# A fused attention and feed-forward block: all first loads on SP's queue, q and k weights in one transfer, masks set as words, one memset left out

## The chip, the cores and the metric

The kernel runs on one core of one Trainium2 chip. The metric is the device time of one execution in microseconds. A core has five engines with an instruction stream each: TensorE (PE in the profile, its weight loads PEld), VectorE (DVE), ScalarE (ACT), GpSimd (POOL) and SyncE (SP, used here for issuing transfers). Transfers are carried out by 16 DMA engines; SP and ACT each have a queue of their own into them (SPq and ACTq in the profile).

## The reference

```python
x = A_x                                    # 1 x 2048 x 448, bf16
xn = _layernorm(x, axis=-1)
return x + _A_ref(xn, A_wqkv, A_wo) + _B_ref(xn, B_w_gate, B_w_up, B_w_down)

def _A_ref(x, wqkv, wo):                   # H = 16 heads of Dh = 28, window W = 256
    qkv = (lambda x, *d: x.transpose(*d))((x @ wqkv).reshape(B, S, 3, H, Dh), 2, 0, 3, 1, 4)
    q, k, v = qkv[0], qkv[1], qkv[2]
    scores = jnp.einsum("bhqd,bhkd->bhqk", q, k) * (Dh ** -0.5)
    mask = (idx[:, None] - idx[None, :] >= 0) & (idx[:, None] - idx[None, :] < W)
    ...
    return (lambda x, *d: x.transpose(*d))(o, 0, 2, 1, 3).reshape(B, S, D) @ wo

def _B_ref(x, w_gate, w_up, w_down):       # F = 1792
    return (_gelu(x @ w_gate) * (x @ w_up)) @ w_down
```

A layer norm of 2048 tokens with 448 features, then two branches from it: attention over a sliding window of 256 tokens, and a gated feed-forward layer. Both are added to the input.

## The kernel before

Tokens are cut into 16 tiles of 128 and into four blocks of 512 (`qb` 0 to 3). All weights stay in SBUF. A block runs through projection of q, k and v, attention (scores, exponential, masking, product with v), the gate and up products with the gelu between them, and the down product, which ends with the add of x and a store. The stages of neighbouring blocks are interleaved by a plan written out by hand; nothing is reordered by a scheduler, so each engine runs its instructions in the order in which the program states them, and each queue issues its transfers in that order.

The change touches the start. What happens there, with lines:

- Lines 85 to 98 issue the first loads. Tile 0 of x goes to SP's queue (L85), tile 1 to ACT's (L86), tiles 2 and 3 to SP's in one transfer (L87). The q and k weights (`wraw`, rows 0 to 383 of `A_wqkv`) come in parts: the first four heads of q and of k on ACT's queue (L89), the other twelve later on SP's (L97). Between them SP issues the v weights (`wv`, L90), the last 64 weight rows, twice, into both halves of the partitions (L92 for q and k, L94 for v), and tiles 4 to 7 of x (L95). The first part of the up weights (`wu`) follows (`load_ffn`, L82).
- Line 124 sets `warm` (the later home of `wo`) to zero in two memsets: the first 512 columns, which the warm-up matmuls read, and the rest. Line 134 sets the masks to 1.
- L717 runs nine matmuls on the zeros (`warmup(9)`), L729 a tenth.
- L718 to 739 take tiles 0 to 3 through statistics (L155, L156, VectorE), the inverse deviation (L160, L161, ScalarE), the normalisation (L170, VectorE) and the transpose (L184 and L186, TensorE; the copy out of PSUM L187, on ScalarE for tiles 0 to 2, on VectorE for tile 3). In between, the first v products run (L191), and the pad copies (L711) spread the first heads' weights from `wraw` to slots of 32 columns in `wqp` (VectorE) and `wkp` (ScalarE).
- L745 and 746 are the first q and k products, on all four tiles; L747 copies the last weight rows to `w3p`; L750 to 752 take the statistics of tiles 4 and 5; L244 and L245 copy q and k out; L652 and L656 are scores and exponential.

Further on, in `ahead3` (L778 to 797), SP issues a list of later loads: the gate weights, the rest of the up weights, tiles 12 to 15 of x in one transfer (L789), `wo` in eight, and the down weights (`wd`, L797) in four transfers of up to four row blocks.

Of the kernel before, what the change touches and what calls it, by code (L numbers as in the profile page):

```python
# [13 lines left out]
f32 = mybir.dt.float32  # L14
i32 = mybir.dt.int32

S, D, H, Dh, F = 2048, 448, 16, 28, 1792
P = 128
NT = S // P
NF = F // P  # L20
QB, NB = 512, 4
# [6 lines left out]
def kernel(  # L28
# [11 lines left out]
    nc = tc.nc  # L40
# [18 lines left out]
    xv = A_x.rearrange("b (n p) d -> p (b n) d", p=P)  # L59
# [3 lines left out]
    x_sb = const.tile([P, NT, D], bf16, name="x_sb")  # L63
    wv = const.tile([P, 4, D], bf16, name="wv")
    v_sb = const.tile([P, NT, H, 32], bf16, name="v_sb")
    wraw = blk.tile([P, 4, 2 * D], bf16, name="wraw", tag="hT")
# [5 lines left out]
    def rows(w, c0, n):  # L72
        return w[c0 * P:(c0 + n) * P, :].rearrange("(c p) n -> p c n", p=P)

    def load_ffn(dst, w, pairs):

        wv64 = w.rearrange("(c p) (h n) -> p c h n", p=64, h=2)
        ns = slice(pairs.start * P, pairs.stop * P)  # L80
        for hi in range(2):
            nc.sync.dma_start(out=dst[64 * hi:64 * hi + 64, :, ns], in_=wv64[:, :, hi, ns])  # L82

    wqk = rows(A_wqkv, 0, 3)[:, :, 0:2 * D]
    nc.sync.dma_start(out=x_sb[:, 0, :], in_=xv[:, 0, :])  # L85
    nc.scalar.dma_start(out=x_sb[:, 1, :], in_=xv[:, 1, :])  # L86
    nc.sync.dma_start(out=x_sb[:, 2:4, :], in_=xv[:, 2:4, :])  # L87
    for c in (0, D):
        nc.scalar.dma_start(out=wraw[:, 0:3, c:c + 4 * Dh], in_=wqk[:, :, c:c + 4 * Dh])  # L89
    nc.sync.dma_start(out=wv[:, 0:3, :], in_=rows(A_wqkv, 0, 3)[:, :, 2 * D:3 * D])  # L90
    for a in range(2):
        nc.sync.dma_start(out=wraw[64 * a:64 * a + 64, 3, 0:D], in_=A_wqkv[384:448, a * D:(a + 1) * D])  # L92
    for a in range(2):
        nc.sync.dma_start(out=wv[64 * a:64 * a + 64, 3, :], in_=A_wqkv[384:448, 2 * D:3 * D])  # L94
    nc.sync.dma_start(out=x_sb[:, 4:8, :], in_=xv[:, 4:8, :])  # L95
    for c in (0, D):
        nc.sync.dma_start(out=wraw[:, 0:3, c + 4 * Dh:c + D], in_=wqk[:, :, c + 4 * Dh:c + D])  # L97
    load_ffn(wu, B_w_up, slice(0, 5))

    ident = const.tile([P, P], bf16, name="ident")  # L100
# [7 lines left out]
    masks = const.tile([P, 3, 4, 64], bf16, name="masks")  # L108
# [11 lines left out]
    eps_t = const.tile([P, 1], f32, name="eps_t")  # L120
    nc.vector.memset(eps_t[:, :], 1e-5)
    warm = wo[:, :, :].rearrange("p g n -> p (g n)")
    for c in (slice(0, QB), slice(QB, 4 * D)):
        nc.vector.memset(warm[:, c], 0.0)
    wqp = const.tile([P, 3, H, 32], bf16, name="wqp")
    wkp = const.tile([P, 3, H, 32], bf16, name="wkp")
    w3p = const.tile([P, H, 32], bf16, name="w3p")
# [3 lines left out]
    nc.vector.memset(wqp[:, :, :, Dh:32], 0.0)  # L131
    nc.vector.memset(wkp[:, :, :, Dh:32], 0.0)
    nc.vector.memset(w3p[:, :, Dh:32], 0.0)
    nc.vector.memset(masks[:, :, :, :], 1.0)
    nc.scalar.preload_act_table_set("natural_log_exp_and_others")

    xnT = const.tile([P, 4, S], bf16, name="xnT")
# [27 lines left out]
    def norm(t):  # L165
        xn = work.tile([P, 4, P], bf16, name="xn", bufs=4)
        xf = xn[:, :, :].rearrange("p a b -> p (a b)")
        both = ((0, D, 0), (D, 64, 384))
        for lo, n, src in both if t > 3 else both[:1]:
            nc.vector.tensor_scalar(out=xf[:, lo:lo + n], in0=x_sb[:, t, src:src + n], scalar1=mv_all[:, t, 0:1],  # L170
                                    scalar2=rstd_all[:, t:t + 1], op0=ALU.subtract, op1=ALU.mult)
        xns[t] = xn

    def dma_transp(t):

        nc.sync.dma_start_transpose(out=xnT[:, :, t * P:(t + 1) * P], in_=xns.pop(t)[:, :, :].rearrange("p a b -> p (a b)"))
# [100 lines left out]
    def fill_pads(last):  # L277


        def put(dst, src, n, lo):  # L280

            src = src.rearrange("p (j d) -> p j d", d=Dh)[:, :, lo:]
            if n == 4:
                nc.gpsimd.tensor_copy(out=dst[:, 12:16, Dh:32], in_=src[:, :, 24:28])
            src = src[:, :, 0:24].rearrange("p j (g i) -> p g j i", i=8)[:, :, :, 0:4]
            nc.gpsimd.tensor_copy(out=dst[:, 0:12, Dh:32].rearrange("p (g j) i -> p g j i", j=4), in_=src)

        if not last:
            for c in range(3):
                k = wraw[:, c, D + 12 * Dh:2 * D]  # L290
                put(wqp[:, c, :, :], k, 4, 0)
                put(wkp[:, c, :, :], k, 3, 4)
            return
        put(w3p[0:64, :, :], w3k[0:64, :], 4, 0)
        put(w3p[64:128, :, :], w3k[64:128, :], 3, 4)
        nc.gpsimd.memset(w3p[64:128, 12:16, :], 0.0)
# [135 lines left out]
    def swap(qb, t=None, n=4):  # L432

        t0 = P * (4 * qb if t is None else t)
        to = t0 - qb * QB + ring(qb).start
        for hi in range(2):
            nc.sync.dma_start(out=xsw[64 * hi:64 * hi + 64, :, to:to + n * P],
                              in_=xnT[64 - 64 * hi:P - 64 * hi, 0:3, t0:t0 + n * P])

    def swap_weights():  # L440

        for hi, src in enumerate((wqp, wkp)):
            nc.sync.dma_start(out=wsq[64 * hi:64 * hi + 64], in_=src[64 - 64 * hi:P - 64 * hi, 0:3])
# [334 lines left out]
    def ahead3():  # L778
        for t in (5, 6, 7):
            norm(t)  # L780
            dma_transp(t)
        swap(1, 4, 2)
        swap(1, 6, 2)
        fill_pads(False)
        swap_weights()
        load_ffn(wg, B_w_gate, slice(0, 3))
        load_ffn(wg, B_w_gate, slice(3, 7))
        load_ffn(wu, B_w_up, slice(5, 7))
        nc.sync.dma_start(out=x_sb[:, 12:16, :], in_=xv[:, 12:16, :])  # L789
        wo_v = A_wo.rearrange("(g j d) n -> j d g n", g=4, j=4)  # L790
        tail = A_wo[14 * Dh:, :].rearrange("(t i) n -> i t n", i=4)
        for j, (t0, n) in enumerate(SLOTS):
            nc.sync.dma_start(out=wo[32 * j:32 * j + Dh, 0:n, :], in_=wo_v[j][:, 0:n])
            nc.sync.dma_start(out=wo[32 * j + Dh:32 * j + 32, 0:n, :], in_=tail[:, t0:t0 + n])
        for k in range(0, NF, 4):
            n = min(4, NF - k)
            nc.sync.dma_start(out=wd[:, k:k + n, :], in_=rows(B_w_down, k, n))  # L797

    for qb in range(NB):
# [4 lines left out]
        if qb == 0:  # L804
# [3 lines left out]
            w = gen_pairs(1, (("v", 0), ("v", 2), ("k", 0), ("k", 1), ("k", 2)))  # L808
            plan = [[(u, 2), ahead, (u, 1)], [lambda: v_dense(2, pvs[2]), (u, 2), ahead2, (u, 1)],
                    [lambda: spare.append(spare.pop(1)), (u, 2), ahead3, (u, 4)], [lambda: stat(8), (u, 11)],  # L810
                    [lambda: stat(9), (u, 7), lambda: stat(10), (u, 7), lambda: fill_pads(True)], ["sums", (u, 7)],
                    ["inverse", "scale", (w, 11)], [(w, 10)],
# [210 lines left out]
```

## Time and profile before

| | |
|---|---|
| device time, median of three runs | 214.37 us (214.35, 214.37, 214.7) |
| span of the profiled execution, first to last instruction | 213.1 us |
| mean granted TensorE clock | 0.996 |
| TensorE busy | 207.6 us, 97% |
| VectorE busy | 157.5 us, 74% |
| ScalarE busy | 131.6 us, 62% |
| GpSimd busy | 48.6 us, 23% |
| bytes moved by DMA | 15.67 MB, mean 74 GB/s |

For the profiled execution the span is known, not a device time of its own. The page has the busy time of each engine, the span in 40 slices, the DMA queues, the chain of work that ended last, and the costliest groups. Queries on the trace give the instructions in order of time, with the idle time of the engine ahead of each and what ended it in square brackets, and the busy time of chosen stretches. A row of SPq or ACTq is the time in which the queue's engine issues a transfer, not that in which the bytes move. Sizes in KB are units of 1024 bytes; GB/s are decimal.

### The profile page before, as it was taken

Reading aid. Unit: us, or ns where it says so; the run is one execution under the profiler, and the core shown is the slowest. Engines: PE = TensorE matmul, PEld = TensorE weight load, DVE = VectorE, ACT = ScalarE, POOL = GpSimd, SP = SyncE. Lnnn points to the kernel's source line nnn. Section 1 sums busy time; section 2 is a strip of 40 time slices with the busy share of each in tenths; the row PEclk is TensorE's granted clock in tenths of the full one; section 3 lists DMA queues with packets and bytes.
Section 4 is the critical chain, followed back from the end, with each engine's and each line's share of the span. In section 5 each row is a group of like instructions: output and inputs, shape, how many; then the busy total and the mean of one; then the engine's idle time right before and its main releaser. Section 6 shows DMA issues by size and latency. Waiting matters only on the chain.

```text
span 213.1 us, 6428 instructions
## 1 busy us (share of the span) xinstructions
PE 207.6 (97%) x2722; PEld 101.2 (47%) x2722; DVE 157.5 (74%) x355; ACT 131.6 (62%) x123; POOL 48.6 (23%) x86
## 2 busy tenths in 40 slices
PE   7999999999999999999999999999999999999992
PEld 2433444444454545444445445444445444544992
DVE  7899998999767985796536997495483898479531
ACT  4699578566777977423777887532676877665000
POOL 5287658451000220041000201022000022006001
PEclk9999999999999999999999999999999999999998
DMA  6999969979420101003421000001000101000011
GB/s 184 280 221 215 106 172 220 243 241 171 110 53 25 37 20 26 8 5 65 74 74 46 25 0 29 20 0 30 16 3 0 47 4 45 6 0 0 26 45 49
DMA packets 23993, 15.67 MB, mean 74 GB/s; under 512 B 9208, under 2 KB 23832, under 8 KB 23960
## 3 DMA queue, kind: packets, MB, share of 16 engines
q1 hardware_dynamic: 22918, 14.87, 31.2%
q8 instruction: 22, 0.36, 0.7%
q10 hardware_dynamic: 1042, 0.34, 0.7%
q14 instruction: 11, 0.09, 0.1%
HBM read 9.26 MB, written 2.41 MB: 55 GB/s over the span
## 4 chain that ended last, share of the span: by engine, by line
PE 94%; DVE 1%; ACT 1%; DMA 1%; issue 1%; DVEq 0%; ACTq 0%
PE po L393 26%; PE gt L456 20%; PE u L456 12%; PE ue L456 8%; PE pq L334 7%; PE sc L652 6%; PE ov L624 5%; PE pv L320 4%; PE pq L191 2%; PE pv L191 1%; DMA x_sb<-in_A_x_dram 1%; ACT p_sb L656 1%; DVE st L155 1%; PE s L191 1%; PE pk L191 1%
## 5 line engine op out<-in xcount | busy, mean ns | idle before, releaser
L656 ACT ACTIVATE p_sb<-sc 128x2048 bf16<-128x2048 f32 x39 | 73.2, 1878 | 20.5 <-PE sc L652 13.5
L496 ACT ACTIVATE p_sb<-gt 128x1024 bf16<-128x1024 f32 x28 | 28.7, 1025 | 33.6 <-PE gt L456 30.7
L591 POOL TENSOR_TENSOR oN<-oc,l 128x512 bf16<-128x512 f32 x16 | 21.5, 1355 | 120.0 <-DVE l L604 120.0
L393 PE MATMUL po<-wd,hT 128*128 128x448 bf16 (+1 forms) x266 | 46.2, 324 | 0.0
L456 PE MATMUL gt<-xnT,wg 64*128 64x512 bf16 x224 | 45.6, 376 | 0.0
L456 PE MATMUL gt<-xsw,wg 64*128 64x512 bf16 x168 | 40.7, 376 | 0.0
L504 DVE TENSOR_TENSOR hT<-p_sb,u 128x512 bf16<-128x512 bf16 x34 | 21.9, 677 | 16.0 <-PE u L456 15.8
L572 DVE TENSOR_TENSOR p_sb<-p_sb,masks 128x256 bf16<-128x256 bf16 (+1 forms) x90 | 27.8, 363 | 7.6 <-ACT p_sb L656 7.6
L393 PEld LDWEIGHTS <-hT 128*128 128x128 bf16 x266 | 24.5, 98 | 16.8 <-issue 2.2
L456 PEld LDWEIGHTS <-wg 64*128 64x128 bf16 x392 | 19.0, 94 | 22.5 <-issue 0.2
L456 PEld LDWEIGHTS <-wu 64*128 64x128 bf16 x392 | 18.7, 94 | 22.4 <-issue 0.8
L456 PE MATMUL u<-xnT,wu 64*128 64x512 bf16 x136 | 28.1, 376 | 0.0
L456 PE MATMUL u<-xsw,wu 64*128 64x512 bf16 x102 | 24.7, 376 | 0.0
L382 DVE TENSOR_TENSOR res<-po,x_sb 128x448 bf16<-128x448 f32 (+1 forms) x17 | 9.8, 592 | 11.6 <-PE po L393 9.3
L456 PE MATMUL ue<-xnT,wu 64*128 64x512 bf16 x88 | 18.0, 377 | 0.0
L652 PE MATMUL sc<-qT,kT 28*64 28x320 bf16 (+7 forms) x648 | 16.4, 261 | 0.1
L456 PE MATMUL ue<-xsw,wu 64*128 64x512 bf16 x66 | 16.4, 377 | 0.0
L582 POOL TENSOR_SCALAR_AFFINE_SELECT p_sb<-p_sb 128x512 bf16<-128x512 bf16 (+1 forms) x21 | 14.2, 702 | 6.6 <-ACT p_sb L656 6.5
L609 DVE TENSOR_TENSOR oc<-oc,ov 128x512 f32<-128x512 f32 x12 | 8.2, 681 | 8.7 <-ACT oc L608 8.7
L652 PEld LDWEIGHTS <-kT 28*64 28x64 bf16 (+1 forms) x648 | 7.5, 102 | 13.3 <-issue 12.0
L393 PE MATMUL po<-wo,oN 128*128 128x448 bf16 (+1 forms) x70 | 13.0, 320 | 0.0
L473 DVE CAST hT<-ue 128x512 bf16<-128x512 f32 x18 | 11.6, 679 | 1.9 <-PE ue L456 1.8
(108 smaller groups left out, 276.9 us busy)
## 6 DMA issues: line engine op xcount, KB each, us to landing
out_dram<-res SPq DMA_DIRECT2D x15, 112.0 KB
x_sb<-in_A_x_dram SPq DMA_DIRECT2D x3, 448.0 KB
wd<-in_B_w_down_dram SPq DMA_DIRECT2D x3, 448.0 KB
xsw<-xnT SPq DMA_DIRECT2D x6, 192.0 KB
wu<-in_B_w_up_dram SPq DMA_DIRECT2D x2, 560.0 KB
wg<-in_B_w_gate_dram SPq DMA_DIRECT2D x2, 448.0 KB
wg<-in_B_w_gate_dram SPq DMA_DIRECT2D x2, 336.0 KB
wraw<-in_A_wqkv_dram SPq DMA_DIRECT2D x2, 252.0 KB
```

The source lines that it names most:

```text
L334: nc.tensor.matmul(ps, lhsT=w.rearrange("p h d -> p (h d)"), rhs=xchunk(qb, hi, c, qb * QB, QB), start=c == 0, stop=c == 6, tile_position= ...
L393: nc.tensor.matmul(po[:, a:b], lhsT=x[:, k, tt * P:(tt + 1) * P], rhs=wt[:, k, lo + a:lo + b], start=start and n == a == 0, stop=stop and ...
L456: nc.tensor.matmul(ps, lhsT=w[64 * hi:64 * hi + 64, c, p * P:(p + 1) * P], rhs=xchunk(qb, hi, c, qb * QB, QB), start=c == 0, stop=c == 6, ...
L473: copy(out=hTs[qb][:, p + 7 * i, :], in_=us[i])
L496: nc.scalar.activation(out=ges[p][:, :, :], in_=gt[:, :, :], func=ACT.Gelu_apprx_tanh)
L504: nc.vector.tensor_tensor(out=hT[:, p + 7 * i, :], in0=ge[:, i, :], in1=u, op=ALU.mult)
L572: nc.vector.tensor_tensor(out=reg, in0=reg, in1=m, op=ALU.mult)
L582: nc.gpsimd.affine_select(out=reg, in_=reg, pattern=mid + [[1 if diag else -1, min(w, P)]], compare_op=ALU.is_ge, fill=0.0, base=0 if diag ...
L591: nc.gpsimd.tensor_tensor(out=oN[:, g, :], in0=oc[:, :], in1=inv, op=ALU.mult)
L624: nc.tensor.matmul(ov[half or 0][32 * j:32 * j + 32, q0:q0 + nq], lhsT=v_sb[r, kt, 4 * g + j, :], rhs=p_sb[r, j, col:col + nq], start=n == ...
L652: nc.tensor.matmul(ss[k0:k0 + nk, j, col:col + nq], lhsT=kT[r, g, kt * P + k0:kt * P + k0 + nk], rhs=qT[r, g, ring(qb).start + q0:ring(qb) ...
L656: nc.scalar.activation(out=p_sb[:, :, 0:ncol], in_=ss[:, :, 0:ncol], func=ACT.Exp, scale=SCALE)
```

## The change

The first loads all go to SP's queue: tile 0, tile 1, tiles 2 and 3, the v weights with their last rows, the q and k weights of rows 0 to 383 in one transfer of whole rows (1792 bytes a row in place of pieces of 224 and 672), their last rows, then tiles 4 and 5, 6 and 7. The masks are set as 32-bit words that hold two bf16 ones each. The second memset of `warm` goes. Later on, tiles 12 to 15 come in two transfers, and the down weights in five, of up to three row blocks.

```diff
     nc.sync.dma_start(out=x_sb[:, 0, :], in_=xv[:, 0, :])
-    nc.scalar.dma_start(out=x_sb[:, 1, :], in_=xv[:, 1, :])
+    nc.sync.dma_start(out=x_sb[:, 1, :], in_=xv[:, 1, :])
     nc.sync.dma_start(out=x_sb[:, 2:4, :], in_=xv[:, 2:4, :])
-    for c in (0, D):
-        nc.scalar.dma_start(out=wraw[:, 0:3, c:c + 4 * Dh], in_=wqk[:, :, c:c + 4 * Dh])
     nc.sync.dma_start(out=wv[:, 0:3, :], in_=rows(A_wqkv, 0, 3)[:, :, 2 * D:3 * D])
     for a in range(2):
+        nc.sync.dma_start(out=wv[64 * a:64 * a + 64, 3, :], in_=A_wqkv[384:448, 2 * D:3 * D])
+    nc.sync.dma_start(out=wraw[:, 0:3, :], in_=wqk)
+    for a in range(2):
         nc.sync.dma_start(out=wraw[64 * a:64 * a + 64, 3, 0:D], in_=A_wqkv[384:448, a * D:(a + 1) * D])
-    for a in range(2):
-        nc.sync.dma_start(out=wv[64 * a:64 * a + 64, 3, :], in_=A_wqkv[384:448, 2 * D:3 * D])
-    nc.sync.dma_start(out=x_sb[:, 4:8, :], in_=xv[:, 4:8, :])
-    for c in (0, D):
-        nc.sync.dma_start(out=wraw[:, 0:3, c + 4 * Dh:c + D], in_=wqk[:, :, c + 4 * Dh:c + D])
+    for t in (4, 6):
+        nc.sync.dma_start(out=x_sb[:, t:t + 2, :], in_=xv[:, t:t + 2, :])
     load_ffn(wu, B_w_up, slice(0, 5))
...
-    for c in (slice(0, QB), slice(QB, 4 * D)):
-        nc.vector.memset(warm[:, c], 0.0)
+    nc.vector.memset(warm[:, 0:QB], 0.0)
...
-    nc.vector.memset(masks[:, :, :, :], 1.0)
+    nc.vector.memset(masks[:, :, :, :].rearrange("p a b c -> p (a b c)").bitcast(f32), 1 + 0x3F80 / 2**23)
...
-        nc.sync.dma_start(out=x_sb[:, 12:16, :], in_=xv[:, 12:16, :])
+        for t in (12, 14):
+            nc.sync.dma_start(out=x_sb[:, t:t + 2, :], in_=xv[:, t:t + 2, :])
...
-        for k in range(0, NF, 4):
-            n = min(4, NF - k)
+        for k in range(0, NF, 3):
+            n = min(3, NF - k)
             nc.sync.dma_start(out=wd[:, k:k + n, :], in_=rows(B_w_down, k, n))
```

## The prediction

> **What bounds the kernel now.** I read the page's shares first, then the busy time of the stretch in which TensorE works, then the chain of waits from the front, then the engines' first rows in order of time. In the second answer the columns are the stretch, its length, busy time by engine with instruction counts, granted clock, DMA share and GB/s.
>
> ```profile
> PE 207.6 (97%) x2722; PEld 101.2 (47%) x2722; DVE 157.5 (74%) x355; ACT 131.6 (62%) x123; POOL 48.6 (23%) x86
> ```
> ```profile
> 1.40:209.60 208.20, 207.54 (x2722) 101.14 (x2722) 157.13 (x352) 131.62 (x123) 47.12 (x78) 1.00 0.33 75
> ```
>
> Between 1.4 and 209.6 us TensorE is busy for all but 208.20 - 207.54 = 0.66 us. Transfers, VectorE and ScalarE therefore cannot win time by being faster in the body of the kernel; there they can only lose it, by being late. One stretch hides more than that row shows, because matmuls without use count as busy: the start.
>
> ```profile
> 0.82 2.45 DMA x_sb<-in_A_x_dram
> ...
> 3.29 0.64 DVE st L155
> ```
> ```profile
> 1.39 4.02 PE L150 MATMUL wps<-wo 128*128 128x512 bf16 x9 [1.39 <-DVE wo L124]
> 5.20 0.53 PE L184 MATMUL tp<-ident,xn 128*128 128x128 bf16 x3
> ...
> 5.91 0.61 PE L150 MATMUL wps<-wo 128*128 128x512 bf16 x1
> 6.31 0.40 PE L184 MATMUL tp<-ident,xn 128*128 128x128 bf16 x3
> 6.64 0.25 PE L186 MATMUL tp<-ident,xn 128*64 128x128 bf16 x2
> 6.99 0.74 PE L191 MATMUL pv<-wv,xnT 128*128 128x448 bf16 x3
> ```
> ```profile
> 9.05 0.33 PEld L191 LDWEIGHTS <-wqp 128*128 128x128 bf16 x3 [0.29 <-DVE xnT L187]
> ```
>
> The chain opens with the load of x tile 0: issued at 0.82, landed 2.45 us later, at 3.27. From there VectorE normalises four tiles in a row. TensorE runs nine matmuls that nobody reads, from 1.39 on, then transposes each tile as it comes. It meets its last visible wait at 9.05, for the copy of tile 3's transpose. So in this kernel a change of the first loads is worth what it does to the time of that 9.05, and nothing else.
>
> ```profile
> 1.06 0.94 DVE L124 MEMSET wo<- 128x256 uint32 x2
> 2.37 0.70 DVE L134 MEMSET masks<- 128x768 bf16 x1
> 3.29 0.63 DVE L155 BATCH_NORM_STATS2 st<-x_sb 128x6 f32<-128x448 bf16 x1 [0.23 <-DMA x_sb<-in_A_x_dram]
> 4.05 0.59 DVE L155 BATCH_NORM_STATS2 st<-x_sb 128x6 f32<-128x448 bf16 x1
> 5.06 0.62 DVE L155 BATCH_NORM_STATS2 st<-x_sb 128x6 f32<-128x448 bf16 x1
> ...
> 7.84 0.27 DVE L711 COPY wqp<-wraw 128x336 bf16<-128x336 bf16 x1
> 8.57 0.42 DVE L187 COPY xnT<-tp 128x512 bf16<-128x512 bf16 x1 [0.46 <-PE tp L186]
> 9.10 0.62 DVE L155 BATCH_NORM_STATS2 st<-x_sb 128x6 f32<-128x448 bf16 x1
> 10.91 0.69 DVE L245 CAST kT<-s 128x512 bf16<-128x512 f32 x1 [0.24 <-PE s L197]
> ```
>
> These are VectorE's rows. Only the first statistics row waits for a transfer, and for 0.23 us.
>
> **The change, part by part.** *The memsets.* The two of L124 set 256 + 640 words in 0.94 us; the 640 go, which by words is 0.94 x 640 / 896 = 0.67 us. The masks' 768 halves become 384 words; at 0.94 / 896 us a word that is 0.40 in place of 0.70 us. VectorE is then free at about 3.07 - 0.67 - 0.30 = 2.1 us rather than at 3.07. By itself this is worth nothing: the load of x tile 0 covers it. But it is needed for the next part, since with VectorE busy until 3.07 an earlier tile could win 0.22 us at most. The first memset, which releases TensorE at 1.39, is the same.
>
> *Tile 1 and the weights leave ACT's queue.*
>
> ```profile
> 0.82 0.42 ACTq L86 DMA_DIRECT2D x_sb<-in_A_x_dram  x1
> 1.27 1.01 ACTq L89 DMA_DIRECT2D wraw<-in_A_wqkv_dram  x2
> 2.31 1.28 ACT L135 ACT_TABLE_LOAD   x1 [2.31 <-issue]
> 4.17 0.29 ACT L160 ACTIVATE lnv<-mv_all,eps_t 128x1 f32<-128x1 f32 x1 [0.58 <-DVE mv_all L156]
> ```
> ```profile
> 0.82 0.39 SPq L85 DMA_DIRECT2D x_sb<-in_A_x_dram  x1
> 1.27 0.42 SPq L87 DMA_DIRECT2D x_sb<-in_A_x_dram  x1
> 1.74 0.47 SPq L90 DMA_DIRECT2D wv<-in_A_wqkv_dram  x1
> 2.24 1.21 SPq L92 DMA_DIRECT2D wraw<-in_A_wqkv_dram  x2
> 3.50 1.23 SPq L94 DMA_DIRECT2D wv<-in_A_wqkv_dram  x2
> 4.77 0.59 SPq L95 DMA_DIRECT2D x_sb<-in_A_x_dram  x1
> ```
>
> Today tiles 0 and 1 are issued in the same moment from two queues and share the engines. Afterwards tile 0 has them alone. ScalarE's table load ends at 3.59 now and its first work starts at 4.17, so the 1.5 us of issuing it is spared is covered. What tile 0 gains, no row shows. The nearest is a store of the same 112 KB at the kernel's quiet end, where the result buffer's next writer waits for it:
>
> ```profile
> 204.88 3.89 SPq L384 DMA_DIRECT2D out_dram<-res  x4
> ```
> ```profile
> 206.73 0.62 DVE L382 TENSOR_TENSOR res<-po,x_sb 128x448 bf16<-128x448 f32 x1 [1.11 <-DMA out_dram<-res]
> ```
>
> That is 1.85 us from issue to use. So tile 0 lands between 0.82 + 1.85 = 2.67 (a gain of 0.6) and 3.27 (none, if the 2.45 is the latency of a first load). I take 3.0, a gain of 0.27, nearer the middle: the load shares with 112 KB only, and the stream is slow then (133 GB/s in the row of 1.5 to 2.5 us below).
>
> The Trainium skill, "DMA: Bandwidth & Descriptors", section "Queues, rings and completion order", says that each DMA engine takes turns between the queues that have work for it, a packet at a time. By it tile 1 delays tile 0 today, which is the gain taken here; how much, the two rows above must say. The same page, "Issuing engines are not separate DMA queues", speaks against the change: issuing from several engines saves issue time and nothing else. By it the change gives up one issue step for tile 1 and gains nothing in bandwidth; the sum would then be that of the first rival, no gain. The rows of before cannot tell the two apart.
>
> Tile 1 is now issued second on SP, at 1.27. With 1.85 to 2.45 us it lands at 3.1 to 3.7; VectorE wants it at 4.05 - 0.27 = 3.78. Tiles 2 and 3 go to 1.74 and are wanted at 5.06 - 0.27 = 4.79, 3 us later. Neither is waited for.
>
> *Weights in one transfer.* This is the part that can lose. VectorE's pad copy (7.84) reads the first heads of the q weights. They came early, in 168 KB; now the whole 672 KB must land, behind four x tiles, the v weights and their two halves. SP's steps are 0.45, 0.47 and 0.50 us and, for transfers of 64 rows, (4.77 - 3.50) / 2 = 0.63, so the seventh transfer is issued at 0.82 + 2 x 0.45 + 0.47 + 0.50 + 2 x 0.63 = 3.95. Bytes up to its end: 448 + 336 + 112 + 672 KB = 1568 KB = 1.606 MB.
>
> ```profile
> 1.50:2.50 1.00, 1.00 (x3) 0.32 (x3) 0.89 (x5) 0.19 (x1) 1.00 (x2) 1.00 0.56 133
> 2.50:3.50 1.00, 1.00 (x4) 0.31 (x3) 0.77 (x2) 1.00 (x1) 1.00 (x2) 1.00 1.01 305
> 3.50:5.50 2.00, 2.00 (x8) 0.72 (x6) 1.93 (x6) 1.09 (x5) 0.17 (x1) 1.00 1.06 298
> 7.00:9.00 2.00, 2.00 (x16) 1.05 (x16) 1.22 (x5) 1.82 (x5) 0.00 (x0) 1.00 1.11 354
> 11.00:18.00 7.00, 6.88 (x54) 2.55 (x53) 6.43 (x17) 6.57 (x9) 6.00 (x17) 1.00 1.12 229
> ```
>
> By 2.5 us 0.133 MB are through. The other 1.473 MB take 4.16 us at 354 GB/s, 4.94 at 298, 6.43 at 229. To the last byte I add 0.45 us until the landing is seen: tiles 0 and 1, 0.229 MB, are through at 2.5 + 0.096 / 0.305 = 2.82, and tile 0 counts as landed at 3.27. So the weights land at 7.1, 7.9 or 9.4. I take 7.9, from the row of the same kind of transfers. The pad copy may slip until 8.57 - 0.27 = 8.30 before it holds up the copy of tile 3, since VectorE idles 0.46 us there; with the gain of 0.27 that is 8.03. So nothing is lost at 7.9, with 0.13 us to spare. Issue is not the limit: at 298 GB/s the 0.918 MB ahead end at 5.1, after the weights' issue.
>
> Behind them come the last weight rows (112 KB) and tiles 4 and 5 (224 KB): 1.95 MB, by the same working 2.5 + 6.1 + 0.45 = 9.05, wanted at 9.10 - 0.27 = 8.83. VectorE then is 0.22 us late, and the row at 10.91 has 0.24 us of idle time to take it. If that cover is gone, the scores, which need this cast, start later one for one. The loads behind (tiles 6 and 7, the up weights) have the same bytes ahead of them as before.
>
> *Later splits.* Tiles 12 to 15 in two, the down weights in five rather than four: two more issues of about 0.5 us on SP.
>
> ```profile
> 43.02 2.05 SPq L797 DMA_DIRECT2D wd<-in_B_w_down_dram  x4
> 45.17 8.58 SPq L176 DMA_TRANSPOSE xnT<-xn  x4
> ```
> ```profile
> 52.73 2.76 PE po L393 x14
> ```
>
> The down weights are issued until 45.1 and first read at 52.73; one step more leaves over 7 us. Behind them on SP stand the four transposes of tiles 8 to 11, the first at 45.17; their issue is spread over 8.58 us, so an added 0.5 us at its front is small against the gaps between them. Price: none, and 0.5 us if something in that list has no slack after all.
>
> **The sum**, against the profiled span of 213.1: -0.27 at the first tile, 0 for memsets, table load, tile 1 and later splits, +0.05 for weights that come just late: -0.22, span 212.9. The three runs have a median of 214.37, 1.27 more than the span; what lies outside it does not change. Forecast 214.15.
>
> **The rivals.** *Nothing is gained* (0.18): the 2.45 us is latency, tile 1 cost tile 0 nothing; for it, tile 0 is the first load of all; against it, two loads of 112 KB in one moment at 133 GB/s. Time 214.37, with the weights still in time. *The weights come late* (0.20): the one mechanism that ends slower. It needs a landing after 8.30 plus 0.43, that is a mean rate below 1.473 / (8.73 - 0.45 - 2.5) = 255 GB/s from 2.5 us on; for it, 229 in the row from 11 to 18 us and the skewed finish of many engines; against it, that row carries loads into 64 partitions each, these go into 128. At 8.9 the price is 0.6 us: 214.97; at 9.4, 1.1. *The tile comes much sooner* (0.22): landing at 2.67 as the store does. VectorE is free at 2.1, so its whole chain moves by 0.6. TensorE's nine matmuls still end at about 5.2 and the tenth at 6.3, so the v product at 6.99 can come no earlier than the last transposes ahead of it allow, which go at 6.64, so about 6.75; but the waits between 7 and 9.05 close too, and 9.05 moves by 0.45 to 0.55: 213.87, if the weights land by 7.9. *TensorE is the limit* of any gain belongs to the forecast: it caps 6.99 at 0.24, not 9.05.
>
> **How the numbers follow.** Forecast 0.40, no gain 0.18, late 0.20, much sooner 0.22. A change within 0.2% of 214.37, that is 0.43 us, cannot be told from none here. The forecast and the no-gain case lie inside it: same 0.58, faster 0.22, slower 0.20. The forecast's own range is 213.95 to 214.4. The range of 8 in 10 reaches into both outer cases: 213.8 to 214.9.
>
> **What would show it.** In the changed profile the first statistics row should start at 3.0 (2.7 to 3.3) with a longer wait for x_sb ahead of it; the pad copy of wqp should show no wait for wraw, or one whose size gives the loss; the weight load at 9.05 should stand near 8.8; the statistics row of tile 4 should not wait over 0.25 us. I am wrong if 9.05 moves by more than 0.5 us either way, or if it moves and the end does not.

## The result and the profile after

The changed kernel takes 215.86 us (median of 8 executions, 215.35 to 218.48), the kernel before beside it 214.53 us (8 executions, 214.35 to 215.18). The ratio is 1.0073, with a 95% interval of 1.0046 to 1.0099: 1.0 to 2.1 us slower. Forecast were 214.15 us, and 213.8 to 214.9 as the range. One execution of the experiments below, the 219.31 us of e8, was in a slower state and is left out of its ratio.

The head of the page after, and its busy times:

```profile
span 213.7 us, 6426 instructions
...
PE 207.9 (97%) x2722; PEld 101.3 (47%) x2722; DVE 156.7 (73%) x354; ACT 131.6 (62%) x123; POOL 48.5 (23%) x86
```

TensorE does the same work. What has moved is the start. First VectorE's rows in order of time (start, duration, line, operation; in brackets the idle time before it and what ended it):

```profile
1.61 0.38 DVE L131 MEMSET masks<- 128x384 f32 x1
2.83 0.63 DVE L152 BATCH_NORM_STATS2 st<-x_sb 128x6 f32<-128x448 bf16 x1 [0.83 <-DMA x_sb<-in_A_x_dram]
...
3.89 0.63 DVE L152 BATCH_NORM_STATS2 st<-x_sb 128x6 f32<-128x448 bf16 x1 [0.22 <-DMA x_sb<-in_A_x_dram]
...
9.35 0.28 DVE L708 COPY wqp<-wraw 128x336 bf16<-128x336 bf16 x1 [1.55 <-DMA wraw<-in_A_wqkv_dram]
9.54 0.41 DVE L184 COPY xnT<-tp 128x512 bf16<-128x512 bf16 x1
9.87 0.27 DVE L744 COPY w3p<-wraw 128x448 bf16<-128x448 bf16 x1
...
10.63 0.63 DVE L152 BATCH_NORM_STATS2 st<-x_sb 128x6 f32<-128x448 bf16 x1 [0.48 <-DMA x_sb<-in_A_x_dram]
...
12.12 0.66 DVE L242 CAST kT<-s 128x512 bf16<-128x512 f32 x1
```

Tile 0 is there at 2.83 and not at 3.29, as meant. But the pad copy of the q weights, at 7.84 before, stands at 9.35 and has waited 1.55 us for `wraw`. Behind it, in VectorE's order, stands the copy of tile 3's transpose (L184, 8.57 before, 9.54 now), and behind that the statistics of tile 4, which wait 0.48 us more (9.10 before, 10.63 now) and push the cast of k (10.91 before, 12.12 now). TensorE's rows show both:

```profile
7.02 0.76 PE L188 MATMUL pv<-wv,xnT 128*128 128x448 bf16 x3
...
10.01 0.82 PE L188 MATMUL s<-xnT,wqp 128*128 128x512 bf16 x3 [0.76 <-DVE xnT L184]
...
12.83 0.40 PE L649 MATMUL sc<-qT,kT 28*128 28x128 bf16 x8 [0.17 <-DVE kT L242]
```

The first q product is 0.96 us later than before (9.05). The first scores began at 11.66 before and are 1.17 later. From there on the shift stays: the last long stretch of the down product began at 195.31 before, and in the chain of waits after it stands at

```profile
196.48 13.88 PE po L390 x126
```

which is 1.17 again. So the loss is made in the first 13 us, and on balance nothing is added or given back in the 180 us that follow. (The two spans, 213.1 and 213.7, differ by 0.6 only; the ends differ too, of which the last experiments tell.)

Now the transfers. The issue of the q and k weights on SP's queue, and five stretches (as in the prediction: length, busy times, clock, DMA share, GB/s):

```profile
3.97 0.59 SPq L91 DMA_DIRECT2D wraw<-in_A_wqkv_dram  x1
```
```profile
1.50:2.50 1.00, 1.00 (x3) 0.32 (x3) 0.46 (x3) 0.60 (x1) 1.00 (x2) 1.00 0.50 135
2.50:3.50 1.00, 1.00 (x4) 0.31 (x3) 0.64 (x2) 0.00 (x0) 1.00 (x2) 1.00 0.88 167
3.50:5.50 2.00, 2.00 (x8) 0.82 (x6) 1.75 (x5) 0.99 (x4) 0.16 (x1) 1.00 1.06 314
5.50:7.00 1.50, 1.50 (x11) 0.72 (x8) 1.43 (x6) 1.13 (x4) 0.00 (x0) 1.00 0.94 261
7.00:9.00 2.00, 2.00 (x18) 1.08 (x16) 0.49 (x2) 1.40 (x4) 0.00 (x0) 1.00 1.05 317
```

Summed up, 0.135 + 0.167 + 2 x 0.314 + 1.5 x 0.261 = 1.322 MB are through at 7.0 us, and the 1.606 MB to the end of the weights at 7.0 + 0.284 / 0.317 = 7.9 us. Yet VectorE gets the weights at 9.35. The trace has a semaphore event for each of the 16 DMA engines that take part in a transfer; this is when the first and the last of them had finished:

```text
                          after: issued  first  last     before: issued  first  last
x tile 0                   0.82          2.54   2.80      0.82           2.70   3.27
x tile 1                   1.27          2.97   3.87      0.82           2.89   3.44
x tiles 2, 3               1.73          4.05   4.77      1.27           3.58   4.26
v weights, 336 KB          2.20          5.17   5.90      1.74           5.13   6.43
first heads, q / k         -                              1.27, 1.76     3.97   4.49 / 5.35 6.86
q and k weights, 672 KB    3.97          7.95   9.32      -
other heads, q / k         -                              5.40, 6.87     8.83   9.54 / 9.50 10.54
tiles 4, 5                 5.78          9.29  10.60      4.77 (4 to 7)  7.89   8.71
```

The first engine is done with its sixteenth of the weights at 7.95, when the sum of the bytes says so; the last one 1.37 us later, and only then does the transfer count. Fifteen of the sixteen parts are down by 8.80, so the last 0.52 us are the wait for one part alone; of tiles 4 and 5 fifteen are down by 9.83 and the last one at 10.60. The trace also lists each packet with its size, and the 384 packets of 1792 bytes are the rows of this transfer: the first starts at 5.35, 1.38 us after the issue, 376 are through by 8.02, and the last one at 8.70.

### The profile page after: what moved, and what is told of

The parts are those of the page before. It is cut to its first block, busy times and chain, and to the rows that moved or that the text cites. A ratio compares the mean times of both kernels' runs of the same rounds, so it can differ in the third digit from the quotient of the medians.

```text
span 213.7 us, 6426 instructions
## 1 busy us (share of the span) xinstructions
PE 207.9 (97%) x2722; PEld 101.3 (47%) x2722; DVE 156.7 (73%) x354; ACT 131.6 (62%) x123; POOL 48.5 (23%) x86
## 4 chain that ended last, share of the span: by engine, by line
PE 91%; DMA 2%; SPq 2%; DVE 1%; ACT 1%; issue 1%; DVEq 0%; ACTq 0%
PE po L390 26%; PE gt L453 20%; PE u L453 12%; PE ue L453 8%; PE pq L331 7%; PE sc L649 6%; PE ov L621 5%; PE pv L317 4%; DMA x_sb<-in_A_x_dram 2%; PE pq L188 2%; ACT p_sb L653 1%; PE pk L188 1%; SPq L90 1%; DVE st L152 1%; SPq L93 1%
```

## The experiments

Each kernel stands beside executions of the kernel before on the same chip, which give its ratio. Three theories stood at the start: that the whole rows are the cause, since the first heads' 168 KB now arrive with 504 KB which nobody needs before 11.5 us (A); that the single queue is the cause (C); and that the small parts, memsets and late splits, carry some of it. In the second set F is the theory that a TensorE left idle at the start gets its full clock later in some executions, and G that in these the loads land later.

### The whole rows alone (e5)

The kernel before, tile 1 still on ACT's queue, with the weights in one transfer on SP ahead of tiles 4 to 7:

```diff
-    for c in (0, D):
-        nc.scalar.dma_start(out=wraw[:, 0:3, c:c + 4 * Dh], in_=wqk[:, :, c:c + 4 * Dh])
...
+    nc.sync.dma_start(out=wraw[:, 0:3, :], in_=wqk)
     nc.sync.dma_start(out=x_sb[:, 4:8, :], in_=xv[:, 4:8, :])
-    for c in (0, D):
-        nc.sync.dma_start(out=wraw[:, 0:3, c + 4 * Dh:c + D], in_=wqk[:, :, c + 4 * Dh:c + D])
```

> The kernel before with the single transfer alone: ACT's queue keeps tile 1, but the q and k weights of rows 0 to 383 come whole on SP's queue ahead of tiles 4 to 7. Theory A: pad copy waits until 9 us or later, first q product at about 10, 215.2 to 215.9. Rival C (the single queue costs): within 0.4 us of before.

Measured: 217.31 us (215.81 to 218.19), ratio 1.0134 (1.0096 to 1.0172). VectorE's rows:

```profile
3.32 0.63 DVE L152 BATCH_NORM_STATS2 st<-x_sb 128x6 f32<-128x448 bf16 x1 [0.26 <-DMA x_sb<-in_A_x_dram]
...
9.23 0.28 DVE L708 COPY wqp<-wraw 128x336 bf16<-128x336 bf16 x1 [1.28 <-DMA wraw<-in_A_wqkv_dram]
...
10.79 0.63 DVE L152 BATCH_NORM_STATS2 st<-x_sb 128x6 f32<-128x448 bf16 x1 [0.77 <-DMA x_sb<-in_A_x_dram]
```

The pad copy waits as in the changed kernel, the scores start at 12.99 (11.66 before), and tile 0 comes at its old time. So the loss is there without the single queue, and C isn't needed for it; the time is above what A had forecast. But it isn't the same wait over again. The transfer is issued at 4.77 here and not at 3.97, it has the last rows of q and k ahead of it too (112 KB more), and the stream was thin just before:

```profile
5.50:7.00 1.50, 1.09 (x10) 0.48 (x8) 1.43 (x6) 0.97 (x4) 0.00 (x0) 1.00 0.76 136
```

By the same sum as above the 1.720 MB are through at 8.6 us. The weights land at 9.21, only 0.6 us later, and their 16 parts within 0.39 us of each other. Here the bytes themselves are late, and the last part adds little.

### The one transfer cut in two, q ahead of k (e4)

```diff
-    nc.sync.dma_start(out=wraw[:, 0:3, :], in_=wqk)
+    for c in (0, D):
+        nc.sync.dma_start(out=wraw[:, 0:3, c:c + D], in_=wqk[:, :, c:c + D])
```

> The changed kernel with its one transfer cut in two of 336 KB, q then k, same place, same bytes, same order. Theory A: the q pad copy waits for half the bytes, so it goes at about 8.3 instead of 9.35, the k pad copy on ScalarE at about 9.3; first q product at about 9.3, time 214.6 to 215.2. Rival D (one DMA engine of the 16 is late by over 1 us whatever the size): the q pad copy still goes after 9.0 and the time stays at 215.4 or more.

Measured: 215.69 us (215.38 to 218.08), ratio 1.0063 (1.0037 to 1.0090). VectorE's rows:

```profile
7.91 0.28 DVE L709 COPY wqp<-wraw 128x336 bf16<-128x336 bf16 x1 [0.36 <-DMA wraw<-in_A_wqkv_dram]
...
9.62 0.28 DVE L745 COPY w3p<-wraw 128x448 bf16<-128x448 bf16 x1 [0.69 <-DMA wraw<-in_A_wqkv_dram]
...
10.16 0.63 DVE L153 BATCH_NORM_STATS2 st<-x_sb 128x6 f32<-128x448 bf16 x1 [0.25 <-DMA x_sb<-in_A_x_dram]
```

With half the bytes the pad copy comes 1.44 us sooner, and the first q product at 8.99, ahead of before's 9.05. So the bytes in the transfer are a part of what the pad copy waits for, and a copy after 9.0 whatever the size, as rival D had it, is out. The lag behind the stream is not: by the sum of the bytes (1.262 MB) the q half is through at 6.8, and it lands at 7.88, 1.05 us later, the last of its parts 0.33 us behind the fifteenth. The time is above A's forecast and where D had it, since most of the loss is still there: the copy of the last weight rows, which are issued behind the k half, waits 0.69 us, tile 4 waits 0.25 more, and the scores start at 12.36. The first wait hid a second one.

### The first heads early, on the single queue (e2)

The changed kernel with the heads' two transfers behind tiles 2 and 3, the other heads at the place of the whole rows:

```diff
     nc.sync.dma_start(out=x_sb[:, 2:4, :], in_=xv[:, 2:4, :])
+    for c in (0, D):
+        nc.sync.dma_start(out=wraw[:, 0:3, c:c + 4 * Dh], in_=wqk[:, :, c:c + 4 * Dh])
...
-    nc.sync.dma_start(out=wraw[:, 0:3, :], in_=wqk)
+    for c in (0, D):
+        nc.sync.dma_start(out=wraw[:, 0:3, c + 4 * Dh:c + D], in_=wqk[:, :, c + 4 * Dh:c + D])
```

> The changed kernel, but the q and k weights in four transfers again: the first four heads of each, 84 KB, right behind x tiles 2 and 3, the other heads in the place of the single transfer; all on SP's queue. Theory A: the pad copy no longer waits, the 1.2 us at the first q product come back, and the earlier tile 0 (2.83 against 3.29) stays, so 214.1 to 214.5, at or under before. Rival C (what costs is the single queue, not the single transfer): the pad copy or the first statistics of tiles 1 to 3 still wait, 215 or more.

Measured: 216.77 us (216.44 to 219.19), ratio 1.0133 (1.0069 to 1.0196). TensorE's rows, then VectorE's:

```profile
7.17 0.73 PE L191 MATMUL pv<-wv,xnT 128*128 128x448 bf16 x3 [0.83 <-DMA wv<-in_A_wqkv_dram]
...
13.04 0.40 PE L652 MATMUL sc<-qT,kT 28*128 28x128 bf16 x8 [1.01 <-DVE kT L245]
```
```profile
7.42 0.27 DVE L711 COPY wqp<-wraw 128x336 bf16<-128x336 bf16 x1
...
10.44 0.28 DVE L747 COPY w3p<-wraw 128x448 bf16<-128x448 bf16 x1 [1.28 <-DMA wraw<-in_A_wqkv_dram]
```

The pad copy waits for nothing now, and the kernel is no faster: 168 KB put ahead of the v weights make the v product wait 0.83 us, and the last weight rows, still behind all the heads, come 1.28 us late. In its simple form, that the pad copy's wait is the loss, A falls too. (The time is the one set for C, but the pad copy and the statistics of tiles 1 to 3, which C named, wait for nothing.) What is lost is the order: in before only what is needed by 9 us is ahead of tiles 4 to 7.

### The other heads last (e6, e7)

The changed kernel with the heads early as in e2 and the other heads moved behind tiles 4 and 5; in e7 the first heads go to ACT's queue, stated behind the table load. Of e6's edit, the part that differs from e2:

```diff
-    nc.sync.dma_start(out=wraw[:, 0:3, :], in_=wqk)
...
-    for t in (4, 6):
-        nc.sync.dma_start(out=x_sb[:, t:t + 2, :], in_=xv[:, t:t + 2, :])
+    nc.sync.dma_start(out=x_sb[:, 4:6, :], in_=xv[:, 4:6, :])
+    for c in (0, D):
+        nc.sync.dma_start(out=wraw[:, 0:3, c + 4 * Dh:c + D], in_=wqk[:, :, c + 4 * Dh:c + D])
+    nc.sync.dma_start(out=x_sb[:, 6:8, :], in_=xv[:, 6:8, :])
```

> As the changed kernel with the first four heads' weights behind tiles 2 and 3, but now the other heads' weights (504 KB, first used at about 11.5 us) go behind tiles 4 and 5. All still on SP. Theory E (the loss is bytes that are not needed yet, ahead of bytes that are): with 504 KB less ahead, tiles 4 and 5 are used at about 9.6 instead of 10.83 and the time falls by about 1 us against the variant with the other heads ahead, to 215.0 to 215.8. Rival C (one queue: SP issues nine transfers of 0.5 to 0.6 us ahead of tile 4, whatever their order): v product at 7.17 and tiles 4 and 5 over 10 us as there, 216.3 or more.

Measured: 216.72 us (215.58 to 217.04), ratio 1.0082 (1.0056 to 1.0108). TensorE's rows, to 14 us and from 17 us on:

```profile
7.05 0.73 PE L191 MATMUL pv<-wv,xnT 128*128 128x448 bf16 x3 [0.79 <-DMA wv<-in_A_wqkv_dram]
9.10 0.82 PE L191 MATMUL s<-xnT,wqp 128*128 128x512 bf16 x3
...
11.71 0.40 PE L652 MATMUL sc<-qT,kT 28*128 28x128 bf16 x8
```
```profile
18.91 0.38 PE L456 MATMUL ue<-xnT,wu 64*128 64x512 bf16 x1
19.86 0.39 PE L456 MATMUL ue<-xsw,wu 64*128 64x512 bf16 x2 [0.57 <-DMA xsw<-xnT]
```

The scores are back at 11.71, and tile 4's statistics at 9.30, as E said; the time is still the one that was set for C, because the up product now waits for a transfer that it didn't wait for before: `xsw`, a copy of the normalised tiles within the chip, landed at 17.97 and 18.66 in before and lands at 18.98 and 19.72 here. It stands in the same queue behind the first loads, with the same bytes ahead of it, which took about a microsecond longer. Part of that is the beginning: from 2.5 to 3.5 us 305 GB/s moved in before, 167 after, and in this kernel

```profile
2.50:3.50 1.00, 1.00 (x4) 0.31 (x3) 0.67 (x2) 0.00 (x0) 1.00 (x2) 1.00 0.83 177
```

which is 0.128 MB less than in before, some 0.4 us at 300 GB/s. In e5, where ACT issues tile 1 at 0.82 and nothing else, the row is

```profile
2.50:3.50 1.00, 1.00 (x4) 0.29 (x3) 0.74 (x2) 0.05 (x1) 1.00 (x2) 1.00 1.05 336
```

so it is the early second transfer that fills this microsecond. Where the rest of the delay of `xsw` comes from was not separated. Two figures point to the one queue: SP comes to issue `xsw` at 11.30, and at 10.19 in before; and from 7 to 9 us 208 GB/s moved here, and 354 in before.

> The same order, but the first four heads' weights are issued by ACT behind its table load, at about 2.1 us, when tile 0 is nearly in. Both theories agree that this undoes the loss: statistics of tile 0 at 2.85, no wait of VectorE for weights, first q product at 8.7 to 8.9, time 214.1 to 214.5. If tiles 4 and 5 are still waited for, theory E alone is not enough.

Measured: 216.88 us (215.54 to 217.71), ratio 1.0097 (1.0067 to 1.0127). ACT issued the heads at 0.85, beside the table load and not behind it, and so beside tile 0:

```profile
3.24 0.63 DVE L155 BATCH_NORM_STATS2 st<-x_sb 128x6 f32<-128x448 bf16 x1 [1.25 <-DMA x_sb<-in_A_x_dram]
...
4.00 0.59 DVE L155 BATCH_NORM_STATS2 st<-x_sb 128x6 f32<-128x448 bf16 x1
...
5.78 0.63 DVE L155 BATCH_NORM_STATS2 st<-x_sb 128x6 f32<-128x448 bf16 x1 [0.69 <-DMA x_sb<-in_A_x_dram]
```

So the order that was meant, heads behind the tiles, was not reached. What the kernel shows is two queues sharing the engines: tile 0 at 3.24 and not 2.83, tile 2 late by 0.69. The theories stay undecided by it.

### The whole rows on ACT's queue (e3)

The changed kernel with the one transfer on ACT's queue. It is stated behind the table load, but is issued beside it, at 0.85:

```diff
     nc.sync.dma_start(out=x_sb[:, 2:4, :], in_=xv[:, 2:4, :])
+    nc.scalar.preload_act_table_set("natural_log_exp_and_others")
+    nc.scalar.dma_start(out=wraw[:, 0:3, :], in_=wqk)
...
-    nc.sync.dma_start(out=wraw[:, 0:3, :], in_=wqk)
...
-    nc.scalar.preload_act_table_set("natural_log_exp_and_others")
```

> The changed kernel with its single transfer of 672 KB issued by ACT behind the table load, at about 2.1 us, and not by SP at 3.97; bytes the same. Rival C: most of the loss goes, 214.8 or less. Theory E: the pad copy goes sooner (7.5 to 8.5), but the bytes still stand ahead of tiles 4 and 5 and share the engines with tiles 2 and 3 and the v weights, so the wait moves there: v product or tile 4 waits, 215.0 to 216.0.

Measured: 217.90 us (216.18 to 218.84), ratio 1.0134 (1.0089 to 1.0179). VectorE's rows, and two stretches:

```profile
3.48 0.63 DVE L152 BATCH_NORM_STATS2 st<-x_sb 128x6 f32<-128x448 bf16 x1 [1.48 <-DMA x_sb<-in_A_x_dram]
...
5.57 0.63 DVE L152 BATCH_NORM_STATS2 st<-x_sb 128x6 f32<-128x448 bf16 x1 [1.25 <-DMA x_sb<-in_A_x_dram]
...
9.39 0.27 DVE L708 COPY wqp<-wraw 128x336 bf16<-128x336 bf16 x1
```
```profile
6.00:9.10 3.10, 1.92 (x14) 0.96 (x15) 2.68 (x10) 2.02 (x8) 0.00 (x0) 1.00 0.99 295
9.10:12.50 3.40, 3.40 (x17) 1.53 (x16) 2.41 (x8) 1.83 (x5) 1.05 (x5) 0.50 1.02 230
```

The pad copy waits for nothing, but the 672 KB share the engines with the tiles, which come late: tile 1 by 1.25 us. TensorE is busy for 0.66 of the 2 us from 5 to 7 and for 1.92 of the 3.10 us of the first row, and after that it is granted half its clock (0.50) for 3.4 us. The scores start at 14.65, 3.0 us late. Both theories had forecast less.

### Matmuls without use before the first q product (e8)

The changed kernel with three more warm-up matmuls (`warmup(3)`, the same zeros as L717) behind the second v product.

> The changed kernel with three more matmuls on zeros ahead of the first q product, where TensorE stands idle for 0.8 us. About the executions of the changed kernel that are 1 to 3 us over the rest (216.61, 217.54, 218.48 of 8): theory F (idle TensorE delays the moment at which the clock is granted, and so lengthens those executions): none over 216.5. Rival G (the transfers land later in those executions): still 2 or 3 in 10 over 216.5. In either case the fastest executions stay at 215.3 to 215.6, since the three matmuls fit into the wait.

Measured: 216.47 us (215.08 to 219.31), ratio 1.0066 (1.0043 to 1.0089); four of its nine executions took over 216.5 us, the longest 219.31. Keeping TensorE busy didn't bring the long executions down, which speaks against F as their whole cause; more on this below the table. In the profiled execution the pad copy is at 9.07 after a wait of 1.51 us, as in the changed kernel.

### The small parts together, and apart (e1, e9, e10)

e1 is the kernel before with the two trimmed memsets and the late splits; e9 has the memsets alone, e10 the splits alone.

```diff
-    for c in (slice(0, QB), slice(QB, 4 * D)):
-        nc.vector.memset(warm[:, c], 0.0)
+    nc.vector.memset(warm[:, 0:QB], 0.0)
...
-        for k in range(0, NF, 4):
-            n = min(4, NF - k)
+        for k in range(0, NF, 3):
+            n = min(3, NF - k)
```

> The kernel before with only the small parts of the change: the unread memset left out, the masks set as words, tiles 12 to 15 in two transfers, the down weights in five. Theory A (the loss is the late landing of the q and k weights, 9.35 us in the changed profile against use at 7.84 before): these parts are covered, time within 0.4 us of before, first statistics row still at about 3.3 us, weight load of the first q product at about 9.05. Rival B (the later splits or the memsets cost the time): 215.5 or more.

> The kernel before with the two memsets trimmed, and nothing else. Run with all the small parts, e1, the scores started 0.14 us earlier than before and the time was still 0.4 us longer. If the late splits carry that 0.4, this kernel is 0.0 to 0.2 us faster than before (scores at 11.5, ratio 0.999 to 1.000). If the memsets carry it, by whatever means, it is 0.3 to 0.5 us slower and the late splits alone are neutral.

> The kernel before with tiles 12 to 15 in two transfers and the down weights in five, and nothing else. If the late splits carry the 0.4 us of e1, the start is that of before (scores at 11.66) and the time is 0.3 to 0.5 us over it. If they are free, as the prediction had it, the ratio is 0.999 to 1.001.

Measured: e1 214.94 us, ratio 1.0019 (1.0007 to 1.0031); e9 214.68 us, 1.0007 (0.9994 to 1.0020); e10 215.27 us (214.81 to 217.08), 1.0040 (1.0020 to 1.0059). The memsets are worth nothing, as forecast. The splits, which were forecast at nothing, cost 0.4 to 1.3 us. Where? In the chain of waits of e10:

```profile
195.31 13.88 PE po L393 x126
```

To the hundredth the row of before. Its body loses nothing; what it loses lies behind the last matmul. There SP waits, one after the other, for the eight semaphores that its transfers signal in rotation, and then for them again with other engines' in the same order. These are SP's semaphore events, read from the trace:

```text
before  211.54  semaphore 7 of 8       e10  211.26  semaphore 1 of 8
        211.69  last store landed           211.46  last store landed
        211.70  semaphore 8 of 8            211.47  semaphore 2 of 8
        211.77  second list begins          211.56, .64, .71, .79, .85, .92  semaphores 3 to 8
        213.08  end (1.39 after landing)    211.99  second list begins
                                            213.30  end (1.84 after landing)
```

Two more transfers move the last store from the eighth semaphore to the second, and six waits of about 0.075 us, that were over before the landing, now stand behind it. The other kernels bear it out: from the last landing to the end of the span it is 1.39 or 1.40 us in all whose last store is on the eighth (before, after, e3, e8, e9, e11), 1.60 on the fifth (e5), 1.75 or 1.76 on the third (e2, e6, e7), 1.84 on the second (e1, e10), and 1.93 on the first (e4). (The next expectation counts to an event 0.03 us ahead of the end.)

### Eight transfers more (e12)

Late splits as in e10, and six stores in the middle of the kernel in two halves each:

```diff
-            nc.sync.dma_start(out=outv[:, t, lo:up], in_=res[:, 0:w])
+            for a, b in ((0, w // 2), (w // 2, w)) if 4 <= t < 10 else ((0, w),):
+                nc.sync.dma_start(out=outv[:, t, lo + a:lo + b], in_=res[:, a:b])
```

> The kernel before with the late splits of e10, and six stores in the middle of the kernel (tiles 4 to 9) in two halves each. That is eight more transfers on SP than before, where e10 had two. Theory: the late splits cost nothing in the body; they move the last store, by two in a rotation of eight semaphores, from the one that the end of the program waits for last to the one that it waits for second, so that six more waits of 0.075 us stand behind the last landing (1.81 us from there to the end in e10 and e1, 1.36 in before). With eight more transfers the last store is back on the last of the eight: 1.36 us from the last landing to the end, the chain on TensorE unmoved, and a time within 0.2 us of before, though four times as many transfers were added. Rival: the added transfers themselves cost; then this kernel is at least as slow as e10, 0.6 us or more over before, and more by the stores.

Measured: 214.57 us (214.36 to 215.38) beside 214.77 of before, ratio 1.0000 (0.9989 to 1.0010). The head of its page and the last row of its chain of waits:

```profile
span 212.8 us, 6439 instructions
```
```profile
195.28 13.88 PE po L394 x126
```

Its last store lands at 211.42 on the eighth semaphore, and the span ends at 212.81, again 1.39 us later. Eight added transfers cost nothing where two cost 0.4% to the median. That settles the late splits: the price is the place in the rotation, 0.45 us, and not the transfer. What e10's median has beyond that (0.66 us in all) was not separated.

For the change this means: it has two transfers fewer among the first loads (11 in place of 13) and two more later. The last store stays on the eighth semaphore, 1.39 us from the end. So its loss is all in the start.

### The changed kernel again (e11)

> The changed kernel once more, unaltered. If the arrival of the weights is what varies between its executions, the profiled one should again show the pad copy between 9.0 and 9.6 us, with the chain from the scores on shifted by whatever the pad copy is late, and a time of 215.3 to 216.1 for most executions. If its loss is a matter of that one profiled execution, the scores start below 12.2.

Measured: 215.65 us (215.35 to 215.97), ratio 1.0048 (1.0030 to 1.0066). VectorE's row and the chain's:

```profile
9.17 0.28 DVE L708 COPY wqp<-wraw 128x336 bf16<-128x336 bf16 x1 [1.62 <-DMA wraw<-in_A_wqkv_dram]
```
```profile
196.12 13.88 PE po L390 x126
```

The wait is there again; the chain is shifted by 0.81 us here, 1.17 in the first.

### All of them together

The shift of the last matmul's end against before (209.17) and what the rotation adds behind the last landing, from one profiled execution each, beside the ratio's interval times the time before:

| kernel | first q product | first scores | chain | rotation | sum | measured |
|---|---|---|---|---|---|---|
| after | 10.01 | 12.83 | +1.17 | 0 | 1.17 | 1.0 to 2.1 |
| e11 | 9.83 | 12.47 | +0.81 | 0 | 0.81 | 0.6 to 1.4 |
| e1 | 8.91 | 11.52 | -0.14 | +0.45 | 0.31 | 0.2 to 0.7 |
| e2 | 9.22 | 13.04 | +1.38 | +0.37 | 1.75 | 1.5 to 4.2 |
| e3 | 11.58 | 14.65 | +3.00 | 0 | 3.00 | 1.9 to 3.8 |
| e4 | 8.99 | 12.36 | +0.71 | +0.54 | 1.25 | 0.8 to 1.9 |
| e5 | 9.89 | 12.99 | +1.33 | +0.21 | 1.54 | 2.1 to 3.7 |
| e6 | 9.10 | 11.71 | +0.99 | +0.36 | 1.35 | 1.2 to 2.3 |
| e7 | 9.78 | 12.39 | +0.73 | +0.37 | 1.10 | 1.4 to 2.7 |
| e8 | 9.73 | 12.34 | +0.68 | 0 | 0.68 | 0.9 to 1.9 |
| e9 | 9.09 | 11.70 | +0.24 | 0 | 0.24 | -0.1 to 0.4 |
| e10 | 9.04 | 11.65 | 0 | +0.45 | 0.45 | 0.4 to 1.3 |
| e12 | 9.02 | 11.62 | -0.03 | 0 | -0.03 | -0.2 to 0.2 |

Ten of thirteen sums lie within what was measured. In e5, e7 and e8 the profiled execution was among the shortest of its kernel, and the sum is below the interval. What the longer executions do (up to 218.48 us in the changed kernel) has no trace, but their mean granted clock is on record. In e3's trace it is 0.992, and that is the one stretch at half the clock (0.5 x 3.4 / 215.9 = 0.008). It is 0.992 as well in the two longest executions of the changed kernel (217.54 and 218.48) and in the three longest of e7, and 0.989 in the longest of e8, which has the added matmuls; the short ones have 0.994 to 1.000. So these lost clock, as F has it, by estimate about 1.7 us each (0.008 x 215.9), though when they lost it is not on record. Others were as long with their clock kept: 0.998 to 1.000 in the three longer executions of e5 (216.89 to 218.19), 1.000 at 218.08 us in e4. What those do stays open; G was not seen directly. No version beats both kernels: e9 and e12 are level with before, all others are slower.

## Why the prediction was wrong

**The failed step is the landing of the weights, "7.1, 7.9 or 9.4. I take 7.9"; it was 9.32.** The issue was right (3.95 forecast, 3.97 measured). Two terms were mis-sized. The smaller is the rate: 298 GB/s put the 1.606 MB through at 7.44, and they were through at 7.9, mostly because the single queue moved 167 GB/s from 2.5 to 3.5 us where the row of before has 305. The larger is "To the last byte I add 0.45 us until the landing is seen": it was 1.42 (9.32 - 7.9), and by the same sum 1.15 in e11 and 1.12 in e8, which load in the same order. The 0.45 was taken from tiles 0 and 1, the first loads on empty engines, whose 16 parts finish within 0.57 and 0.55 us of each other in before. The parts of these weights finish 1.37 us apart, and already those of the v weights in the trace of before 1.30 (5.13 to 6.43), where it could have been read. The place in the list alone doesn't decide it: in e5, with more bytes ahead of them, the weights finish within 0.39 us. And 0.52 of the 1.37 us is one part behind fifteen others. Why that part is late, the runs don't show.

The Trainium skill, "DMA: Bandwidth & Descriptors", section "Why a DMA increments its semaphore by 16 and not by 1", says that the engines of a transfer finish independently and that only the full count means that all has landed. The trace agrees, with 7.95 for the first and 9.32 for the last.

**"Issue is not the limit"** set the moment of issue, 3.95, against 5.1, when the bytes ahead would be through. The first packet of the weights starts 1.38 us after the issue, at 5.35, and from 5.5 to 6.0 us only 138 GB/s moved. The sum had no term for this.

**"Nothing is lost at 7.9, with 0.13 us to spare"** fell with the landing: the pad copy might slip to 8.03, or 8.30 without the gain, and came at 9.35. *The weights come late* (0.20) is what happened, at the place and by the mechanism it named, "the skewed finish of many engines" among what spoke for it; it priced a landing at 9.4 with 1.1 us, and the chain moved by 1.17. That the two are so close is in part luck: the first q product moved by 0.96, and the rest came from tile 4.

**"a change of the first loads is worth what it does to the time of that 9.05, and nothing else"** was too narrow: in e4 the first q product is at 8.99, and the chain is 0.71 us longer.

**Tiles 4 and 5** were forecast 0.22 us late, within a cover of 0.24 us. They landed at 10.60, not 9.05, again with one part far behind the rest (9.29 to 9.83, and 10.60), and tile 4's statistics moved by 1.53 us. This is the second part of the loss: from 0.96 us at the first q product to 1.17 at the scores. It isn't there in every execution: in e8, with the same order of loads, tile 4 is not waited for, and the shift is 0.68 us at both places.

**Tile 0** came at 2.83, nearer to *The tile comes much sooner* (2.67) than to the forecast's 3.0, and at 2.80 to 2.93 in the five other kernels that load it alone ahead of the rest on SP. The gain is real and worth nothing: with the weights late in VectorE's order there is nobody to hand it on. Of the waits called absent, tile 1's was 0.22 us in one execution and none in the other.

**The memsets** took 0.27 us for the 256 words and 0.38 for the masks, and left VectorE free at 1.99 (2.1 forecast). "By itself this is worth nothing" is what e9 shows.

**The later splits**, "Price: none", were right for the changed kernel, and right of the list on SP that they lengthen. The reason given was not enough: by themselves they cost 0.45 us at the very end, a place the prediction didn't look at, and in the changed kernel two transfers saved at the start cancel it.

That issuing from two engines gains no bandwidth was left as what the rows of before could not tell. From 2.5 to 3.5 us it does not hold (305 against 167 GB/s; a second transfer is under way sooner). Over the first 18 us the mean is 231 GB/s in before, 222 after the change and 210 in e6; how much of that is the second queue was not separated.

## What to carry to other kernels

A load that is waited for counts when the slowest of its 16 parts is down. Behind the sum of the bytes that was 0.6 us in e5 and 1.4 us after the change, so give this lag a range, read from loads that stand as deep in the list and not from the first of all. Keep the piece that is needed first a transfer of its own, with nothing ahead of it that is needed later, as the kernel before does; no version here did better. When one wait at such a start is mended, look at once for the next in the list (e4, e2 and e6 each uncovered another), because the whole list is one stream of bytes. And when the number of transfers changes, compare what lies behind the last landing separately from the chain of work, or an edit is blamed that costs nothing where it stands.

## What the runs showed of the hardware

**The end moves with an instruction load.** In every kernel the third last store and the second last take longer from issue to landing than those ahead of them: in before 3.89 and 3.04 us, behind two of 1.73 and 1.70. The last one takes 2.06 us there, and 1.54 after the change. Of the third last 15 of the 16 parts are down between 208.87 and 209.06, and one at 211.28; the second is alike; the last is held at its issue in before, which takes 0.85 us in place of 0.33. In the same stretch there is one packet of kind "instruction" of 16 KB (the queues of before, 208 to 213 us: packets, MB, share of 16 engines):

```profile
q8 instruction: 1, 0.02, 2.1%
```

That is 0.021 x 16 x 5 = 1.7 us on one engine. In all fourteen traces the late part lands 1.1 to 1.3 us after that packet's end; four of them:

```text
kernel     instruction packet      late part lands   last store: issue to landing
before     208.45 to 210.10        211.28            2.06
after      209.63 to 210.70        211.82            1.54
e10        208.58 to 209.86        211.05            1.84
e11        210.09 to 211.04        212.34            2.40
```

The Trainium skill, "Runtime: NRT & Kernel Launch", section "Instruction fetch mechanics", says that instructions come in blocks of 16 KiB through a DMA queue of their own and that this is mostly hidden. The trace shows the block. Here, at the end, it doesn't look hidden: the late part follows it in every trace, and the last store's time differs between executions by up to 0.86 us (1.54 to 2.40). This is why the span of one profiled execution says less than its chain: after has a chain 1.17 us longer than before and a span only 0.6 longer. That the late part waits for the packet, on the same DMA engine, is not shown; the trace doesn't name the engine.

**Half the clock after a thin start.** In e3 TensorE, busy for 0.66 of the 2 us from 5 to 7 us and for 1.92 of the 3.1 us from 6 us on, was granted 0.50 of its clock for 3.4 us. The thinnest 2 us near the start of other traces left it at 1.00: 0.93 busy in e2 (from 12 us on), 0.99 in e11 (from 8 us on), 1.24 after the change. One drop among fourteen traces doesn't say where the line is, or whether it is the share that decides.
